# Attention products on two 64-row tiles of the matmul array, with chained passes and a reordered tail

## Chip, cores and metric

The kernel runs on one core of a Trainium2 chip. The metric is the device time of one execution in microseconds (us). The engines are named as in the profile: PE (TensorE, matmuls; PEld are its weight loads), DVE (VectorE), ACT (ScalarE), POOL (GpSimd), SP (SyncE, which only issues transfers here). Each works through its own list of instructions in order.

## The reference

```python
def _A_ref(x, k_cache, v_cache, wq, wo):          # 32 heads of 192, D = 640, Sq = Sk = 2048
    W = min(4096, max(256, Sk // 4))              # 512
    q = (x @ wq).reshape(B, Sq, Hq, Dh).transpose(0, 2, 1, 3)
    k, v = k_cache[:, :, Sk - W:, :], v_cache[:, :, Sk - W:, :]
    p = softmax(einsum("bhqd,bhkd->bhqk", q, k) * Dh ** -0.5)
    return einsum("bhqk,bhkd->bhqd", p, v) ... @ wo
def _B_ref(x, w_gate, w_up, w_down):              # F = 1536
    return (sigmoid(x @ w_gate) * (x @ w_up)) @ w_down
xn = layernorm(x)
out = x + _A_ref(xn, ...) * silu(_B_ref(xn, ...))
```

Inputs and output are bfloat16, sums are kept in float32.

## The kernel before

**Opening and gated block.** The 2048 rows are four blocks of 512 (`TB`), each four tiles of 128. Rows are normalised tile by tile (`stats_half`, `stats_end`, `normal`) and turned into `xnT`, on PE for the first block (`turn_pe`; the copies out of PSUM are L233 on DVE and L235 on ACT), by DMA for the others. `tile_gates` (L299) computes the first gates of block 0 tile by tile as the rows come; `gated` (L249) and `down` (L261) do the rest of the gated block and leave `gate`, the silu factor, for all rows. The loads of the opening are issued on SP and, the first gate weights alone, on ACT. At the end of this part the queries of the first two units are computed (L368), on all 128 rows of the array.

**Units.** The attention is cut into 32 units: 8 groups of 4 heads times 4 blocks of 512 queries; unit u is group `u // 4`, block `u % 4`. Each unit needs

- queries (`queries`, L420, evicted by DVE at L427): the contraction over 640 is done in halves of 64 rows, one on each half of the array, the two writing to the two 512-column halves of a PSUM bank pair. In a second pass the halves are exchanged. Between the passes DVE reads one column of the result into a tiny tile `seen` (L425), so that the second pass cannot begin before the first has landed;
- scores (`scores`, L402): heads of 192 in three pieces of 64, again two heads on the two halves of the array; ACT takes the exponential into `E` (L406);
- values (`values`, L436): the exponentials against `vbuf` (192 columns and one column of ones, 193), 16 matmuls a head on the whole array; DVE divides by the sum (L441, L442) into `o_st`;
- the turn of `o_st` into `oT` by four DMA transposes on SP (`turn_out`, L448);
- the projection (`project`, L475): for each of four row tiles, 6 chunks times (512 + 128) columns on the whole array, added by DVE into `acc` (L480, L482). For the last group but one, POOL also loads the row of x (L485, its own DMA queue), multiplies `acc` by `gate` (L486) and adds the row (L487). For the last group `finish_rows` multiplies the projection by `gate` into `o_sb` on DVE (L454; two buffers), adds `acc` (L455, on DVE or POOL) and issues the output (L456).

There are four PSUM bank pairs `bank[0..3]`, 1024 columns each. All of the order is written out by hand (manual schedule): every engine's list follows the order of the Python code.

**Main loop** (L494). 15 iterations of two units u0, u0+1. In the first half of each iteration the scores of these two units alternate with the passes of the queries of units u0+2, u0+3 (scores in banks 0 and 1, queries in 2 and 3); then come, in the second half, for eight heads in turn, one `values` and one `project` (of units u0-2, u0-1; none in the first iteration). The loads of the next group's wq, keys and values are issued on POOL, those of wo on SP.

**Tail** (L523). The scores of units 30 and 31 come in stretches of 6, 6 and 4, with the projections of unit 28 between them, two and two, their additions on DVE and outputs issued on POOL; then the projections of unit 29 (likewise), the values of 30 and 31, the projections of 30, and those of 31 in two halves of 320 columns (L467), each half finished by itself; these last additions are on POOL, for the last row tile on DVE.

Of the kernel before, what the change touches and what calls it, by code (L numbers as in the profile page):

```python
# [9 lines left out]
ALU = mybir.AluOpType  # L10
BF16 = mybir.dt.bfloat16
F32 = mybir.dt.float32
# [3 lines left out]
def kernel(  # L16
# [13 lines left out]
    nc = tc.nc  # L30
    P = 128
    H2 = 64

    xf = A_x.flatten_outer_dims()
# [36 lines left out]
    def wide(i):  # L71
        return bank[i][:].rearrange("p b n -> p (b n)")
# [17 lines left out]
    grp = {}  # L90
# [52 lines left out]
    with ExitStack() as bctx:  # L143
# [8 lines left out]

        xt = {}

        def load_x(t, n):

            x = xpool.tile([P, n, D], BF16, name=f"x_sb{n}", bufs=4 if n == 1 else 2)
            nc.sync.dma_start(x[:], xf[t * P:(t + n) * P, :].rearrange("(q p) d -> p q d", p=P))  # L158
            for i in range(n):
                xt[t + i] = x[:, i, :]  # L160

        def load_f(eng, w, r, f0, f1, c0=0, c1=NCD):
            eng.dma_start(w[:, c0:c1, f0 * P:f1 * P], r[:, c0:c1, f0 * P:f1 * P])

        nc.vector.memset(warm[:], 0.0)

        nc.vector.memset(wg_sb[:, 0, 0:2], 0.0)
        load_x(0, 1)
        load_x(1, 1)
        load_f(nc.scalar, wg_sb, wg_r, 0, 4)  # L170
        load_f(nc.sync, wu_sb, wu_r, 0, 4, 0, 3)
        load_x(2, 1)
        load_f(nc.sync, wu_sb, wu_r, 0, 4, 3, NCD)
# [20 lines left out]
        def stats_half(t, i):  # L194
            if i == 0:
                ln[t] = bwork.tile([P, 2, nc.vector.BN_STATS_DIM], F32, name="st")
            nc.vector.bn_stats(ln[t][:, i, :], xt[t][:, i * (D // 2):(i + 1) * (D // 2)])
# [15 lines left out]
        def normal(t, parts=((0, D),)):  # L213
            mv, rstd = ln[t]
            xn = xpool.tile([P, D], BF16, name="xn")
            for d0, d1 in parts:
                nc.vector.tensor_scalar(xn[:, d0:d1], xt[t][:, d0:d1], mv[:, 0:1], rstd[:, 0:1],
                                        op0=ALU.subtract, op1=ALU.mult)
            ln[t] = xn

        def turn_pe(t):

            engs = (nc.vector, nc.scalar) if t == 0 else (nc.scalar, nc.scalar)
            parts = []
            for i, (c0, c1) in enumerate(((0, 3), (3, NCD))):
                bk = bank[3][:, t % 2, :] if t or i == 0 else bank[2][:, 0, :]
                pT = bk[:, 0:NCD * H2].bitcast(BF16).rearrange("p (c n) -> p c n", c=NCD)
                for c in range(c0, c1):
                    nc.tensor.transpose(pT[:, c, :], ln[t][:, c * P:(c + 1) * P], ident[:])  # L229
                parts.append((engs[i], xnT[:, 0, c0:c1, t * P:(t + 1) * P], pT[:, c0:c1, :]))  # L230
            for eng, dst, src in parts:
                if eng is nc.vector:
                    nc.vector.tensor_copy(dst, src)  # L233
                else:
                    nc.scalar.activation(dst, src, AF.Copy)  # L235
# [75 lines left out]
        stats_half(0, 1)  # L311
        stats_end(0)
        normal(0, ((0, 3 * P), (3 * P, D)))
        turn_pe(0)
        dummy(2)
        stats_half(1, 1)
        stats_end(1)
        stats_half(2, 0)
        normal(1)
        stats_half(2, 1)  # L320
        stats_end(2)
        stats_half(3, 0)
# [67 lines left out]
    NU = NG * NB  # L390
    E = {}
    oT = {}
    seen = acc_pool.tile([P, DJ, 2], F32, name="seen")
    load_wo(0)

    def scores(u, pr, c, k):
# [32 lines left out]
    o_st = {}  # L429

    def values(u, h, k):
        e = E[u, h // 2]
        o4 = wide(k).rearrange("p (q n) -> p q n", q=TQ)
        for q in range(TQ):
            for c in range(KC):
                nc.tensor.matmul(o4[:, q, 0:DH + 1], lhsT=e[:, c, h % 2, q * P:(q + 1) * P],  # L436
                                 rhs=vbuf[:, h, c, 0:DH + 1], start=(c == 0), stop=(c == KC - 1))
        if h == 0:
            o_st[u] = o_pool.tile([P, TQ, GW], BF16, name="o_st")
        rden = small.tile([P, TQ, 1], F32, name="rden")  # L440
        nc.vector.reciprocal(rden[:], o4[:, :, DH:DH + 1])  # L441
        nc.vector.tensor_tensor(o_st[u][:, :, h * DH:(h + 1) * DH], o4[:, :, 0:DH],  # L442
                                rden[:].to_broadcast([P, TQ, DH]), ALU.mult)

    def turn_out(u):
        oT[u] = oT_pool.tile([P, GC, TB], BF16, name="oT")
        for q in range(TQ):
            nc.sync.dma_start_transpose(oT[u][:, :, q * P:(q + 1) * P], o_st[u][:, q, :])  # L448

    def finish_rows(t, d0, d1, src, add, out_eng):  # L450

        o_sb = fin.tile([P, D], F32, name="o_sb", bufs=2)[:, d0:d1]
        r_sb = gate[:, t, d0:d1]
        nc.vector.tensor_tensor(o_sb, src, r_sb, ALU.mult)  # L454
        add.tensor_tensor(r_sb, o_sb, acc[:, t, d0:d1], ALU.add)  # L455
        out_eng.dma_start(of[t * P:(t + 1) * P, d0:d1], r_sb)  # L456

    def project(u, q, k, out_eng, add=nc.vector):
        g, b = u // NB, u % NB
        wo = grp[g]["wo"]  # L460
        t = b * TQ + q
        if u == NU - 1:

            HD = D // 2
            for i in range(2):
                for cc in range(GC):
                    nc.tensor.matmul(bank[k[i]][:, 0, 0:HD],  # L467
                                     lhsT=oT[u][:, cc, q * P:(q + 1) * P],
                                     rhs=wo[:, cc, i * HD:(i + 1) * HD],
                                     start=(cc == 0), stop=(cc == GC - 1))  # L470
                finish_rows(t, i * HD, (i + 1) * HD, bank[k[i]][:, 0, 0:HD], add, out_eng[i])
            return
        for cc in range(GC):
            for d0, d1 in ((0, 512), (512, D)):
                nc.tensor.matmul(wide(k)[:, d0:d1], lhsT=oT[u][:, cc, q * P:(q + 1) * P],  # L475
                                 rhs=wo[:, cc, d0:d1], start=(cc == 0), stop=(cc == GC - 1))
        if g == NG - 1:
            finish_rows(t, 0, D, wide(k)[:, 0:D], add, out_eng)
        elif g == 0:
            nc.vector.tensor_copy(acc[:, t, :], wide(k)[:, 0:D])  # L480
        else:
            nc.vector.tensor_tensor(acc[:, t, :], wide(k)[:, 0:D], acc[:, t, :], ALU.add)  # L482
        if g == NG - 2:
            x_sb = fin.tile([P, D], BF16, name="row")
            nc.gpsimd.dma_start(x_sb[:], xf[t * P:(t + 1) * P, :])  # L485
            nc.gpsimd.tensor_tensor(acc[:, t, :], acc[:, t, :], gate[:, t, :], ALU.mult)  # L486
            nc.gpsimd.tensor_tensor(acc[:, t, :], acc[:, t, :], x_sb[:], ALU.add)  # L487

    sc = [(pr, c) for pr in range(2) for c in range(KC)]
    order = (2, 3, 0, 1)  # L490
# [3 lines left out]
    for u0 in range(0, NU - 2, 2):  # L494
        g, second = u0 // NB, u0 % NB != 0
        more = g + 1 < NG
        for u in (u0, u0 + 1):
            for i, what in enumerate(((0, 0), (1, 0), (0, 1), (1, 1), (2, 0), None, (2, 1), None)):
                scores(u, *sc[i], i % 2)
                if what is not None:  # L500
                    queries(u + 2, what[0], 2 + (what[0] + u) % 2, what[1])
        if more and not second:
            load_wq(g + 1, nc.gpsimd)
            load_keys(g + 1, nc.gpsimd)
        if more and second:
            turn_keys(g + 1)
        if not more:
            load_wo(g)
        for u in (u0, u0 + 1):
            for q in range(4):  # L510
                if u0 > 0:
                    values(u, q, order[2 * q % 4])
                    project(u - 2, q, order[(2 * q + 1) % 4], nc.sync)
                else:
                    values(u, q, order[q])
            turn_out(u)
        if more and second:
            load_values(g + 1, nc.gpsimd)
        if 0 < g < NG - 1 and not second:
            load_wo(g)  # L520


    u = NU - 2  # L523
    sc = [(v, *s) for v in (u, u + 1) for s in sc]
    for i in range(6):
        scores(*sc[i], order[i % 4])
    for q in range(2):
        project(u - 2, q, q, nc.gpsimd)
    for i in range(6, 12):
        scores(*sc[i], order[(i - 6) % 4])  # L530
    for q in range(2, 4):
        project(u - 2, q, q - 2, nc.gpsimd)
    for i in range(12, 16):
        scores(*sc[i], order[i % 4])
    for q in range(4):
        project(u - 1, q, order[q], nc.gpsimd)
    for v in (u, u + 1):
        for h in range(4):
            values(v, h, order[h])
        turn_out(v)  # L540
    for q in range(4):
        project(u, q, order[q], nc.sync, nc.gpsimd if q < 3 else nc.vector)
    for q in range(4):
        i = 2 * q % 4
        project(u + 1, q, order[i:i + 2], (nc.scalar, nc.sync), nc.gpsimd if q < 3 else nc.vector)


# [28 lines left out]
```

The softmax here doesn't subtract the row's maximum and nothing guards it: scores larger than these inputs give would overflow.

## Time and profile before

| what | us |
|---|---|
| median of 6 runs (lowest to highest) | 927.64 (927.22 to 931.09) |
| the profiled execution | 927.22 |
| its span, first to last instruction | 925.4 |
| PE busy | 914.4 (99%) |
| DVE, ACT, POOL busy | 463.3, 302.7, 139.8 |
| scores L402, queries L420 (busy of the group) | 198.4, 223.7 |
| values L436, projection L475 (busy of the group) | 189.5, 197.9 |
| one iteration of the main loop (start of values 801.30 to 848.53) | 47.23 |
| tail, from its first scores to the end of the last matmuls | 872.3 to 920 |

The granted clock of PE is 0.999 of full speed on average. Busy times of PE are sums over pipelined matmuls, of which each record (376 ns for 512 columns) is longer than the distance from one to the next; distances between starts are what counts. In the timeline a line is a merged run of like instructions: start, duration, engine, source line, operation, tiles, rows of the array, shape and count; in brackets is the idle time of the engine before it and what ended it.

### The profile page before, as it was taken

Reading aid. Unit: us, or ns where it says so; the run is one execution under the profiler, and the core shown is the slowest. Engines: PE = TensorE matmul, PEld = TensorE weight load, DVE = VectorE, ACT = ScalarE, POOL = GpSimd, SP = SyncE. Lnnn points to the kernel's source line nnn. Section 1 sums busy time; section 2 is a strip of 40 time slices with the busy share of each in tenths; the row PEclk is TensorE's granted clock in tenths of the full one; section 3 lists DMA queues with packets and bytes.
Section 4 is the critical chain, followed back from the end, with each engine's and each line's share of the span. In section 5 each row is a group of like instructions: output and inputs, shape, how many; then the busy total and the mean of one; then the engine's idle time right before and its main releaser. Section 6 shows DMA issues by size and latency. Waiting matters only on the chain.

```text
span 925.4 us, 17975 instructions
## 1 busy us (share of the span) xinstructions
PE 914.4 (99%) x7926; PEld 547.9 (59%) x8004; DVE 463.3 (50%) x734; ACT 302.7 (33%) x333; POOL 139.8 (15%) x169
## 2 busy tenths in 40 slices
PE   9999999999999999999999999999999999999997
PEld 6445455465757565656565656566666656565665
DVE  5452522444545454645454545545554545454566
ACT  4222222245151514242424233333324242415240
POOL 1000100011002000200020012001100110175744
PEclk9999999999999999999999999999999999999999
DMA  9310330114424232333433252415251415252625
GB/s 321 78 29 1 89 86 1 43 61 86 86 53 112 77 77 62 103 86 50 88 94 96 43 95 78 111 36 103 77 112 29 110 61 98 67 118 92 109 67 126
DMA packets 162334, 76.68 MB, mean 83 GB/s; under 512 B 140976, under 2 KB 157568, under 8 KB 162256
## 3 DMA queue, kind: packets, MB, share of 16 engines
q1 hardware_dynamic: 154832, 52.72, 26.2%
q0 software_dynamic: 6192, 21.83, 8.1%
q8 instruction: 62, 1.02, 0.5%
q10 hardware_dynamic: 1232, 0.98, 0.3%
q14 instruction: 16, 0.13, 0.1%
HBM read 39.45 MB, written 2.62 MB: 45 GB/s over the span
## 4 chain that ended last, share of the span: by engine, by line
PE 97%; issue 1%; DMA 1%; POOL 0%; DVE 0%; SPq 0%; ACT 0%; DVEq 0%
PE bank L475 22%; PE bank L420 21%; PE bank L436 19%; PE bank L402 18%; PE bank L249 10%; PE bank L261 6%; PE bank L368 1%; PE bank L299 1%; DMA x_sb<-in_A_x_dram 1%; POOL gate L455 0%; DVE o_sb L454 0%; PE bank L229 0%; SPq L158 0%; DVE gate L455 0%; ACT xnT L235 0%
## 5 line engine op out<-in xcount | busy, mean ns | idle before, releaser
L406 ACT ACTIVATE E<-bank 128x1024 bf16<-128x1024 f32 x256 | 255.7, 1024 | 456.8 <-PE bank L402 456.7
L420 PE MATMUL bank<-xnT,wq_sb 64*128 64x512 bf16 x1800 | 223.7, 376 | 0.0
L475 PE MATMUL bank<-wo_sb,oT 128*128 128x512 bf16 (+1 forms) x1288 | 197.9, 296 | 3.0
L402 PE MATMUL bank<-qT,kT 64*128 64x512 bf16 x1536 | 198.4, 376 | 0.0
L436 PE MATMUL bank<-vbuf,E 128*128 128x193 bf16 x2048 | 189.5, 247 | 0.0
L436 PEld LDWEIGHTS <-E 128*128 128x128 bf16 x2048 | 168.6, 98 | 18.0 <-issue 6.4
L427 DVE CAST qT<-bank 128x1024 bf16<-128x1024 f32 x90 | 110.2, 1225 | 128.5 <-PE bank L420 128.5
L475 PEld LDWEIGHTS <-oT 128*128 128x128 bf16 x1488 | 117.3, 98 | 75.4 <-issue 1.3
L420 PEld LDWEIGHTS <-wq_sb 64*128 64x128 bf16 x1800 | 93.1, 100 | 102.2
L402 PEld LDWEIGHTS <-kT 64*128 64x128 bf16 x1536 | 74.0, 94 | 89.8 <-issue 4.8
L442 DVE TENSOR_TENSOR o_st<-bank,rden 128x768 bf16<-128x768 f32 x128 | 122.5, 957 | 4.4
L482 DVE TENSOR_TENSOR acc<-bank,acc 128x640 f32<-128x640 f32 x96 | 79.2, 825 | 43.4 <-PE bank L475 43.2
L118 POOL DMA_DIRECT2D vbuf<-in_A_v_cache_dram x28 | 21.1, 753 | 308.0 <-PE bank L436 305.1
L425 DVE COPY seen<-bank 128x2 f32<-128x2 f32 x90 | 14.4, 159 | 93.8 <-PE bank L420 93.8
L441 DVE RECIPROCAL rden<-bank 128x4 f32<-128x4 f32 x128 | 23.4, 182 | 65.1 <-PE bank L436 65.1
L249 PE MATMUL bank<-xnT,wg_sb 128*128 128x512 bf16 x216 | 54.5, 379 | 0.2
L249 PE MATMUL bank<-xnT,wu_sb 128*128 128x512 bf16 x215 | 54.4, 379 | 0.3
L261 PE MATMUL bank<-wd_sb,hT 128*128 128x128 bf16 (+1 forms) x376 | 52.4, 297 | 0.4
L255 DVE TENSOR_TENSOR hT<-bank,sig 128x512 bf16<-128x512 f32 x44 | 30.3, 689 | 42.8 <-ACT sig L252 42.8
L252 ACT ACTIVATE sig<-bank 128x512 bf16<-128x512 f32 x44 | 26.3, 597 | 68.4 <-PE bank L249 65.3
L261 PEld LDWEIGHTS <-hT 128*128 128x128 bf16 x384 | 29.7, 98 | 23.1
L97 POOL DMA_DIRECT2D wq_sb<-in_A_wq_dram x7 | 6.3, 898 | 221.0 <-PE bank L420 221.0
(55 smaller groups left out, 346.2 us busy)
## 6 DMA issues: line engine op xcount, KB each, us to landing
wo_sb<-in_A_wo_dram SPq DMA_DIRECT2D x7, 960.0 KB, 5.3
wq_sb<-in_A_wq_dram POOLq DMA_DIRECT2D x7, 960.0 KB, 5.9
k_st<-in_A_k_cache_dram POOLq DMA_DIRECT2D x14, 384.0 KB, 5.5
vbuf<-in_A_v_cache_dram POOLq DMA_DIRECT2D x28, 192.0 KB, 3.2
row<-in_A_x_dram POOLq DMA_DIRECT2D x16, 160.0 KB, 2.6
oT<-o_st SPq DMA_TRANSPOSE x128, 2.6
x_sb<-in_A_x_dram SPq DMA_DIRECT2D x3, 640.0 KB, 10.4
wd_sb<-in_B_w_down_dram SPq DMA_DIRECT2D x1, 1920.0 KB, 14.3
```

Source lines behind the costliest of these rows:

```text
L249: nc.tensor.matmul(bank[k][:, half, 0:r1 - r0], lhsT=w[:, c, f * P:(f + 1) * P], rhs=xnT[:, b, c, r0:r1], start=(c == 0), stop=(c == NCD - 1))
L252: nc.scalar.activation(sig[:, 0:r1 - r0], bank[k][:, 0, 0:r1 - r0], AF.Sigmoid)
L255: nc.vector.tensor_tensor(hT[b][:, f, r0:r1], bank[k][:, 1, 0:r1 - r0], sig[:, 0:r1 - r0], ALU.mult)
L261: nc.tensor.matmul(wide(k)[:, d0:d1], lhsT=hT[b][:, f, q * P:(q + 1) * P], rhs=wd_sb[:, f, d0:d1], start=(f == 0), stop=(f == NF - 1))
L402: nc.tensor.matmul(bank[k][:, i, :], lhsT=kT[r, pr, j, c * P:(c + 1) * P], rhs=q[r, pr * DJ + j, :], start=(j == 0), stop=(j == DJ - 1))
L406: nc.scalar.activation(E[u, pr][:, c, :, :], bank[k][:], AF.Exp, scale=scale_qk)
L420: nc.tensor.matmul(bank[k][:, half, :], lhsT=wq[r, c, col:col + DJ * (P - 1) + 1:DJ], rhs=xnT[r, b, c, :], start=(c == 0 and not second), ...
L427: nc.vector.tensor_copy(qT[u][:, 2 * m:2 * m + 2, :], bank[k][:])
L436: nc.tensor.matmul(o4[:, q, 0:DH + 1], lhsT=e[:, c, h % 2, q * P:(q + 1) * P], rhs=vbuf[:, h, c, 0:DH + 1], start=(c == 0), stop=(c == KC ...
L442: nc.vector.tensor_tensor(o_st[u][:, :, h * DH:(h + 1) * DH], o4[:, :, 0:DH], rden[:].to_broadcast([P, TQ, DH]), ALU.mult)
L475: nc.tensor.matmul(wide(k)[:, d0:d1], lhsT=oT[u][:, cc, q * P:(q + 1) * P], rhs=wo[:, cc, d0:d1], start=(cc == 0), stop=(cc == GC - 1))
L482: nc.vector.tensor_tensor(acc[:, t, :], wide(k)[:, 0:D], acc[:, t, :], ALU.add)
```

## The change

1. `values` and `project` are done like `queries`: each product is cut into two halves of 64 rows, which run on the two halves of the array and write to the two halves of the bank pair, in two passes with the halves exchanged; a copy of one column of each half into `seen` stands between the passes. A projection's 640 columns are now twice 320. Both become generators that yield after each pass.
2. `flow` chains them: the first pass of the next job stands before the second pass of this one. `pairs` interleaves two jobs pass by pass.
3. In the first half of an iteration, a pass of the queries now stands ahead of the scores, not behind.
4. The tail: scores of unit 30 alternate with the passes of unit 28's projections (additions now on POOL, outputs on SP), scores of unit 31 with the passes of unit 30's values; then values of 31, projections of 29 and of 30, all chained; then the last rows, still on the whole array, with five of the eight additions on POOL (six before).
5. The opening: the first gate weights go in two parts on SP, tile 1 of x on ACT; a small memset goes; tile 1's second statistics stand ahead of `turn_pe(0)`, its normalisation ahead of tile 2's statistics.

```diff
-        load_x(1, 1)
-        load_f(nc.scalar, wg_sb, wg_r, 0, 4)
+        load_x(1, 1, nc.scalar)
+        load_f(nc.sync, wg_sb, wg_r, 0, 4, 0, 3)
+        load_f(nc.sync, wg_sb, wg_r, 0, 4, 3, NCD)
...
+        stats_half(1, 1)
         turn_pe(0)
         dummy(2)
-        stats_half(1, 1)
         stats_end(1)
+        normal(1)
         stats_half(2, 0)
-        normal(1)
...
     def values(u, h, k):
-        for q in range(TQ):
-            for c in range(KC):
-                nc.tensor.matmul(o4[:, q, 0:DH + 1], lhsT=e[:, c, h % 2, q * P:(q + 1) * P],
-                                 rhs=vbuf[:, h, c, 0:DH + 1], start=(c == 0), stop=(c == KC - 1))
+        for turn in range(2):
+            for qq in range(TQ // 2):
+                for c in range(KC):
+                    for i in range(2):
+                        r = slice(i * H2, (i + 1) * H2)
+                        q = (i ^ turn) * (TQ // 2) + qq
+                        nc.tensor.matmul(o4[:, q, 0:DH + 1],
+                                         lhsT=e[r, c, h % 2, q * P:(q + 1) * P],
+                                         rhs=vbuf[r, h, c, 0:DH + 1],
+                                         start=(turn == 0 and qq == 0 and c == 0),
+                                         stop=(turn == 1 and c == KC - 1), skip_group_check=True)
+            if turn == 0:
+                nc.vector.tensor_copy(seen[:, DJ, :], bank[k][:, :, 0])
+                yield
...
     def project(u, q, k, out_eng=None, add=nc.vector):
+        res = bank[k][:, :, 0:HD]
+        for turn in range(2):
+            for cc in range(GC):
+                for i in range(2):
+                    r = slice(i * H2, (i + 1) * H2)
+                    half = i ^ turn
+                    nc.tensor.matmul(res[:, half, :], lhsT=oT[u][r, cc, q * P:(q + 1) * P],
+                                     rhs=wo[r, cc, half * HD:(half + 1) * HD],
...
+            if turn == 0:
+                nc.vector.tensor_copy(seen[:, DJ + 1, :], bank[k][:, :, 0])
+                yield
...
+    def flow(jobs):
+        before = None
+        for j in jobs:
+            next(j)
+            if before is not None:
+                next(before)
+            before = j
+        next(before)
+
+    def pairs(jobs):
+        for i in range(0, len(jobs), 2):
+            for _ in range(2):
+                for j in jobs[i:i + 2]:
+                    yield next(j)
...
-                scores(u, *sc[i], i % 2)
                 if what is not None:
                     queries(u + 2, what[0], 2 + (what[0] + u) % 2, what[1])
+                scores(u, *sc[i], i % 2)
...
+    passes = pairs([project(u - 2, q, 2 + q % 2, nc.sync, nc.gpsimd) for q in range(4)])
+    for i in range(8):
+        scores(u, *sc[i], i % 2)
+        next(passes)
+    passes = pairs([values(u, h, 2 + h % 2) for h in range(4)])
+    for i in range(8):
+        scores(u + 1, *sc[i], i % 2)
+        next(passes)
+    flow([values(u + 1, h, h) for h in range(4)]
+         + [project(u - 1, q, q, nc.scalar, nc.gpsimd) for q in range(4)]
+         + [project(u, q, q, nc.sync, nc.gpsimd if q < 3 else nc.vector) for q in range(4)])
     for q in range(4):
-        project(u, q, order[q], nc.sync, nc.gpsimd if q < 3 else nc.vector)
-    for q in range(4):
-        i = 2 * q % 4
-        project(u + 1, q, order[i:i + 2], (nc.scalar, nc.sync), nc.gpsimd if q < 3 else nc.vector)
+        last_rows(q)
```

More of the change, by code (lines that the diff above doesn't have):

```diff
@@ L153, with load_x @@
         xt = {}
-        def load_x(t, n):
+        def load_x(t, n, eng=nc.sync):
             x = xpool.tile([P, n, D], BF16, name=f"x_sb{n}", bufs=4 if n == 1 else 2)
-            nc.sync.dma_start(x[:], xf[t * P:(t + n) * P, :].rearrange("(q p) d -> p q d", p=P))
+            eng.dma_start(x[:], xf[t * P:(t + n) * P, :].rearrange("(q p) d -> p q d", p=P))
             for i in range(n):
@@ L165 @@
         nc.vector.memset(warm[:], 0.0)
-        nc.vector.memset(wg_sb[:, 0, 0:2], 0.0)
         load_x(0, 1)
-        load_x(1, 1)
-        load_f(nc.scalar, wg_sb, wg_r, 0, 4)
+        load_x(1, 1, nc.scalar)
+        load_f(nc.sync, wg_sb, wg_r, 0, 4, 0, 3)
+        load_f(nc.sync, wg_sb, wg_r, 0, 4, 3, NCD)
         load_f(nc.sync, wu_sb, wu_r, 0, 4, 0, 3)
@@ L392 @@
     oT = {}
-    seen = acc_pool.tile([P, DJ, 2], F32, name="seen")
+    seen = acc_pool.tile([P, DJ + 2, 2], F32, name="seen")
     load_wo(0)
@@ L443, in values @@
                                 rden[:].to_broadcast([P, TQ, DH]), ALU.mult)
+        if h == 3:
+            turn_out(u)
+        yield
     def turn_out(u):
@@ L448, in turn_out, with cols, finish_rows, project @@
             nc.sync.dma_start_transpose(oT[u][:, :, q * P:(q + 1) * P], o_st[u][:, q, :])
-    def finish_rows(t, d0, d1, src, add, out_eng):
+    HD = D // 2
+    def cols(x):
+        return x.rearrange("p (i n) -> p i n", i=2)
+    def finish_rows(t, d0, d1, form, src, add, out_eng):
         o_sb = fin.tile([P, D], F32, name="o_sb", bufs=2)[:, d0:d1]
         r_sb = gate[:, t, d0:d1]
-        nc.vector.tensor_tensor(o_sb, src, r_sb, ALU.mult)
+        nc.vector.tensor_tensor(form(o_sb), src, form(r_sb), ALU.mult)
         add.tensor_tensor(r_sb, o_sb, acc[:, t, d0:d1], ALU.add)
         out_eng.dma_start(of[t * P:(t + 1) * P, d0:d1], r_sb)
-    def project(u, q, k, out_eng, add=nc.vector):
+    def project(u, q, k, out_eng=None, add=nc.vector):
         g, b = u // NB, u % NB
@@ L461, in project @@
         t = b * TQ + q
[L462 to L476, printed above, removed]
+        res = bank[k][:, :, 0:HD]
[6 more added lines that the diff above has]
+                                     rhs=wo[r, cc, half * HD:(half + 1) * HD],
+                                     start=(turn == 0 and cc == 0),
+                                     stop=(turn == 1 and cc == GC - 1), skip_group_check=True)
+            if turn == 0:
+                nc.vector.tensor_copy(seen[:, DJ + 1, :], bank[k][:, :, 0])
+                yield
         if g == NG - 1:
-            finish_rows(t, 0, D, wide(k)[:, 0:D], add, out_eng)
+            finish_rows(t, 0, D, cols, res, add, out_eng)
         elif g == 0:
-            nc.vector.tensor_copy(acc[:, t, :], wide(k)[:, 0:D])
+            nc.vector.tensor_copy(cols(acc[:, t, :]), res)
         else:
-            nc.vector.tensor_tensor(acc[:, t, :], wide(k)[:, 0:D], acc[:, t, :], ALU.add)
+            nc.vector.tensor_tensor(cols(acc[:, t, :]), res, cols(acc[:, t, :]), ALU.add)
         if g == NG - 2:
@@ L487, in project, with last_rows @@
             nc.gpsimd.tensor_tensor(acc[:, t, :], acc[:, t, :], x_sb[:], ALU.add)
+        yield
+    def last_rows(q):
+        u = NU - 1
+        t = (NB - 1) * TQ + q
+        for i in range(2):
+            k = (2 * q + i) % 4
+            for cc in range(GC):
+                nc.tensor.matmul(bank[k][:, 0, 0:HD], lhsT=oT[u][:, cc, q * P:(q + 1) * P],
+                                 rhs=grp[NG - 1]["wo"][:, cc, i * HD:(i + 1) * HD],
+                                 start=(cc == 0), stop=(cc == GC - 1))
+            finish_rows(t, i * HD, (i + 1) * HD, lambda x: x, bank[k][:, 0, 0:HD],
+                        nc.gpsimd if 2 * q + i < 5 else nc.vector, (nc.scalar, nc.sync)[i])
+    def flow(jobs):
[11 more added lines that the diff above has]
+                    yield next(j)
     sc = [(pr, c) for pr in range(2) for c in range(KC)]
@@ L508 @@
             load_wo(g)
+        jobs = []
         for u in (u0, u0 + 1):
@@ L511 @@
                 if u0 > 0:
-                    values(u, q, order[2 * q % 4])
-                    project(u - 2, q, order[(2 * q + 1) % 4], nc.sync)
-                else:
-                    values(u, q, order[q])
-            turn_out(u)
+                    jobs.append(values(u, q, order[2 * q % 4]))
+                    jobs.append(project(u - 2, q, order[(2 * q + 1) % 4], nc.sync))
+                else:
+                    jobs.append(values(u, q, order[q]))
+        flow(jobs)
         if more and second:
@@ L523 @@
     u = NU - 2
[L524 to L534, printed above, removed]
-    for q in range(4):
[L536 to L540, printed above, removed]
-    for q in range(4):
-        project(u, q, order[q], nc.sync, nc.gpsimd if q < 3 else nc.vector)
-    for q in range(4):
-        i = 2 * q % 4
-        project(u + 1, q, order[i:i + 2], (nc.scalar, nc.sync), nc.gpsimd if q < 3 else nc.vector)
+    passes = pairs([project(u - 2, q, 2 + q % 2, nc.sync, nc.gpsimd) for q in range(4)])
[9 more added lines that the diff above has]
+         + [project(u, q, q, nc.sync, nc.gpsimd if q < 3 else nc.vector) for q in range(4)])
+    for q in range(4):
+        last_rows(q)
 _INS = ['A_x', 'A_k_cache', 'A_v_cache', 'A_wq', 'A_wo', 'B_x', 'B_w_gate', 'B_w_up', 'B_w_down']
```

## Prediction

> **What bounds the kernel now.** I read the page first: busy times, then the chain of work that ended last.
>
> ```profile
> PE 914.4 (99%) x7926; PEld 547.9 (59%) x8004; DVE 463.3 (50%) x734; ACT 302.7 (33%) x333; POOL 139.8 (15%) x169
> ...
> PE 97%; issue 1%; DMA 1%; POOL 0%; DVE 0%; SPq 0%; ACT 0%; DVEq 0%
> ```
>
> TensorE (PE) is the chain almost from end to end, so only what shortens PE's own list, or makes PE wait, moves the time. A share of 99% cannot tell a matmul from a pause inside a run of matmuls, so I went on to the timeline of PE (start, duration of the merged run, engine, line, shapes, count). First a stretch of score and query matmuls, then the tail:
>
> ```profile
> 825.05 0.82 PE L402 MATMUL bank<-qT,kT 64*128 64x512 bf16 x6
> 825.71 1.24 PE L420 MATMUL bank<-xnT,wq_sb 64*128 64x512 bf16 x10
> 826.79 0.81 PE L402 MATMUL bank<-qT,kT 64*128 64x512 bf16 x6
> 827.43 1.24 PE L420 MATMUL bank<-xnT,wq_sb 64*128 64x512 bf16 x10
> ...
> 872.28 4.06 PE L402 MATMUL bank<-qT,kT 64*128 64x512 bf16 x36
> 876.27 3.43 PE L475 MATMUL bank<-wo_last,oT 128*128 128x512 bf16 x23
> 879.64 4.06 PE L402 MATMUL bank<-qT,kT 64*128 64x512 bf16 x36
> ...
> 896.22 10.83 PE L436 MATMUL bank<-vbuf,E 128*128 128x193 bf16 x128
> 906.89 6.68 PE L475 MATMUL bank<-wo_last,oT 128*128 128x512 bf16 x47
> 913.41 6.68 PE L467 MATMUL bank<-wo_last,oT 128*128 128x320 bf16 x48
> ```
>
> From start to start: five pairs of 64-row matmuls of 512 columns take 1.08 us, three take 0.64, so a pair takes **0.2155**; the full-array matmul of 512 columns (L249) takes the same. Values take 10.67/128 = **0.0833** each (193 columns). A projection step of 640 columns takes 6.52/24 = **0.2717**, and 320 columns in the last rows 0.136. So two half-array matmuls together are no faster than one whole one; this change cannot win by pace.
>
> What it can win is the **switch** between the forms. 18 pairs of scores should take 3.88 us; the projections start 3.99 after them: 0.11 lost. The 12 steps back take 3.37 instead of 3.26: 0.11 again. Start times of single matmuls say 0.308 instead of 0.212 at the step to 128 rows (and 0.012 at the next matmul) and 0.152 instead of 0.056 at the step back: 0.10 each on average.
>
> **The change, part by part.** The profiled run took 927.22 us (span 925.4 and 1.8 around it), 0.4 below the median 927.64. I add to 927.2.
>
> *1. No switches.* To 128 rows: 15 iterations and 3 times in the tail; back: after L368, 15 times, 2 in the tail; 36. Two stay (after L368, and into last_rows). 34 x 0.10 = **-3.5** (-3.7 to -3.2).
>
> *2. Pace of the pairs.* A projection has 12 pairs of 320 columns: 12 x 0.136 = 1.63, as 6 x 0.2717 does now. Values have 16 pairs of 193 columns a head where 16 whole matmuls stand, 2048 in all. No row shows a pair so short. Lower end: 193/512 of the 512-column pair, 0.0812, 2048 x 0.0021 = -4.3. Upper end: a load and a matmul come every 0.056 us in the opening (L299: 20 in 1.11); if the two halves took turns at that, 0.112 a pair, +59. In the pairs at hand the two loads start 2 ns apart and both last 94 to 101 ns, beside each other; the nearest row for 193 columns is the whole matmul: 0.0833, **0**.
> [...]
>
> *3. The copies into seen.* 128 for values and 124 for projections at 0.16 us (L425): 40 us more on DVE, which is at 463 of 925. They lie beside PE. In a period of 2.96 us (a head and a projection) DVE does 0.18 + 0.96 + 0.82 + 2 x 0.16 = 2.28. A second pass waits for its copy. DVE takes up a result some 0.2 us after its last matmul; by then it may be evicting the head before, until about 1.37 us into the period, so the copy ends at 1.55, and PE wants it at 2.30. Cover 0.75 us for values, 0.95 for projections: **0**. Were it gone, each head would cost what is missing. With heads alone (first iteration, last unit) DVE needs 1.38 a head against PE's 1.33; over 8 heads 0.4 behind: still covered.
>
> *4. Queries ahead of scores.* The same matmuls. ACT's 1.02 per score group stays ahead of PE, the query banks (2, 3) have long been emptied, and wq is needed 0.65 us earlier, some 17 us after it lands: **0**.
>
> *5. Opening.* The second statistics of tile 1 now stand ahead of the copy L233, which moves from 5.83 to 6.00, and the first gates from 6.25 to about 6.45. In return tile 1's normalisation no longer stands behind x tile 2 (landed 7.48), so its turn comes at 8.21 instead of 8.41, and the second tile starts at 9.24 instead of 9.44. The loads move about as many bytes ahead of x tile 2. **-0.2** (-0.5 to +0.4).
>
> *6. The last rows.* DVE now also does the sixth half's addition (0.5 us) ahead of the seventh's product, POOL one less; the buffers of o_sb (two) still chain DVE to POOL at 0.83 a half: **+0.3** (-0.5 to +1). The outputs go from POOL's queue to SP's and ACT's; behind them on SP stand the transposes of unit 30, ready some 6 us later; on ACT nothing but outputs. oT of unit 31 must wait for the projections of unit 29, and has 5.7 us to land against 2.6.
>
> *7. Where it is paid: unit 28's rows in the tail.* Its additions (L455) move from DVE to POOL. POOL's own timeline from the last iteration on:
>
> ```profile
> 852.55 1.39 POOL L486 TENSOR_TENSOR acc<-acc,gate 128x640 f32<-128x640 f32 x1 [10.45 <-DVE acc L482]
> ...
> 876.46 1.41 POOL L486 TENSOR_TENSOR acc<-acc,gate 128x640 f32<-128x640 f32 x1
> 880.95 1.90 POOL L487 TENSOR_TENSOR acc<-acc,row 128x640 f32<-128x640 f32 x1 [3.08 <-DMA row<-in_A_x_dram]
> 882.80 0.58 POOL L485 DMA_DIRECT2D row<-in_A_x_dram  x1
> 883.39 1.41 POOL L486 TENSOR_TENSOR acc<-acc,gate 128x640 f32<-128x640 f32 x1
> 885.46 1.39 POOL L487 TENSOR_TENSOR acc<-acc,row 128x640 f32<-128x640 f32 x1 [0.65 <-DMA row<-in_A_x_dram]
> ```
>
> POOL is **behind**: its eight rounds (issue a row, multiply, wait, add) last from 852.55 to 886.85, 34.3 us, 14.5 us into the tail that begins at 872.35. One iteration earlier they took 33.3. Today nobody waits for that; after the change unit 28's additions queue behind it. In the new kernel the first round starts 4.74 us after the values phase (first projection done at 3.63, then 1.11 as now), the phase lasts 8 x 2.96 = 23.7, so POOL comes free 4.74 + 33.3 to 34.3 - 23.7 = 14.3 to 15.3 into the tail. Its first addition takes 1.54: 15.9 to 16.9. o_sb has two buffers, so the third product waits for that and ends (0.9) at 16.8 to 17.8. It is what empties bank 2, and bank 2 takes the first values of unit 30, which PE reaches after 8 x (0.647 + 0.815) + 0.647 = 12.35. PE waits 4.5 to 5.4; bank 3 follows one POOL addition later, 0.26 more. **+5.2** (4.5 to 5.7; 3.9 if POOL made its fastest rounds).
>
> *8. The clock after that wait.* PE's last matmul starts at 919.8; then:
>
> ```profile
> 920.00:924.40 4.40, 0.09 (x1) 0.00 (x0) 1.99 (x4) 0.00 (x0) 0.81 (x1) 1.00 0.31 93
> 924.50:925.40 0.90, 0.00 (x0) 0.00 (x0) 0.00 (x0) 0.00 (x0) 0.00 (x0) 0.50 0.00 0
> ```
>
> (the column of 1.00 and 0.50 is the granted clock.) It fell about 4.5 us after the last work, and a wait of 4.5 to 5.4 may just reach that. Coming back: in the opening 256 columns took 0.213 (half pace) and full pace was there at the first gates, 5.1 us after the first matmul; half of that is 2.5. So 0 to 2.5; I take **+1.0**, between fall and no fall.
> [...]
>
> Sum: 927.2 - 3.5 + 0 - 0.2 + 0.3 + 5.2 + 1.0 = **930.0**.
>
> **Rivals.**
> A. *No wait in the tail.* If POOL's rows are done by 10 us into the tail, or DVE finds a free o_sb: 927.2 - 3.5 - 0.2 + 0.3 = **923.8**. For it: the switches are certain. Against it: the backlog of two iterations and the third product's dependence on POOL.
> B. *PE's instructions come too slowly*: the case that is clearly slower. A head and a projection today are 56 loads and matmuls in 2.96 us; afterwards 112, one every 26.5 ns. The densest row, L299, shows 28 ns (two in 0.056). It decides from 26.5 ns on (for the 12 heads without a projection from 1.33/64 = 20.8); at 28 each period takes 3.14, so 112 x 0.17 = 19, the 12 heads add 12 x 0.46 = 5.5, and the wait in the tail shrinks by the longer phase to some 3.8: 927.2 - 3.5 + 0.1 + 24.5 + 3.8 = **952**; at 27 about 940. For it: nothing in the trace is denser. Against it: L299 is held by its 128 columns, so 28 is only what was asked.
> C. *The switch stays*, if the drain belongs to a change of half and not of form: 933.5. Against it: scores and queries alternate halves with no gap.
>
> **Numbers.** Forecast 0.62 (927 to 933.5), A 0.18, B 0.17, C 0.03. What can be told from no change is 0.3%, 924.9 to 930.4. The forecast with the clock kept gives about 929, within; with the fall 930 to 932, mostly beyond: 0.34 same, 0.28 slower. Faster is A less 0.01: 0.17; same 0.35; slower 0.28 + 0.17 + 0.03 = 0.48. The range takes in A, the forecast's ends and the mild part of B: 923.5 to 935.
>
> **What would show it.** 64-row value pairs 0.083 apart and an iteration of 47.0 us instead of 47.23 (steps 1, 2); no PE wait for seen; one PE wait of some 5 us for bank 2, released by DVE's o_sb, which itself waits for POOL's gate, and perhaps PEclk below 9 in the slice after it. I am wrong if value pairs stand clearly over 0.083 apart, or if the tail has no such wait.

## Result, and the profile after

| | us |
|---|---|
| median before / after (38 and 17 runs) | 927.64 / 931.75 |
| ratio of the runs | 1.0042, 95% interval 1.0033 to 1.0051 |
| runs after, lowest to highest | 928.78 to 934.88 |
| the profiled execution after, its span | 933.68, 931.9 |

The change makes the kernel 0.4% slower, and spreads its runs over 6 us (before: 4). The page after, first the busy times, then the chain:

```profile
PE 916.1 (98%) x11522; PEld 630.8 (68%) x11540; DVE 485.3 (52%) x978; ACT 302.4 (32%) x333; POOL 146.3 (16%) x168
...
PE 82%; DMA 6%; issue 5%; POOL 4%; DVE 1%; ACT 0%; POOLq 0%
```

Before, the chain was PE to 97%. Now DMA, POOL and "issue" have 15% of it: the chain that ends last runs for a long stretch over POOL and the rows of x that POOL loads and waits for. The matmuls themselves pace as the whole ones did. PE's timeline of one iteration (start, duration of the run, shapes, count):

```profile
704.21 0.61 PE L401 MATMUL bank<-qT,kT 64*128 64x512 bf16 x4
704.64 0.85 PE L441 MATMUL bank<-vbuf,E 64*128 64x193 bf16 x16
705.31 0.99 PE L489 MATMUL bank<-wo_sb,oT 64*128 64x320 bf16 x12
706.13 1.51 PE L441 MATMUL bank<-vbuf,E 64*128 64x193 bf16 x32
707.46 1.81 PE L489 MATMUL bank<-wo_sb,oT 64*128 64x320 bf16 x24
```

Eight value pairs take 0.67 (0.0833 a pair), six projection pairs 0.82. The values start 0.43 after the last two pairs of scores, which is what two pairs take: nothing is lost on the way in. Before, three pairs of scores, 0.65 by their pace, took 0.74 there:

```profile
706.03 0.81 PE L402 MATMUL bank<-qT,kT 64*128 64x512 bf16 x6
706.77 1.51 PE L436 MATMUL bank<-vbuf,E 128*128 128x193 bf16 x16
```

An iteration takes 47.02 us (751.66 to 798.68 between the starts of values) where it took 47.23. The tail then loses what the loop won. POOL, DVE and PE in the tail, which begins at 870.03 (in brackets the idle time of the engine before, and what ended it):

```profile
885.90 1.39 POOL L506 TENSOR_TENSOR acc<-acc,row 128x640 f32<-128x640 f32 x1 [0.62 <-DMA row<-in_A_x_dram]
887.25 6.00 POOL L475 TENSOR_TENSOR gate<-o_sb,acc 128x640 bf16<-128x640 f32 x4
...
888.80 0.82 DVE L474 TENSOR_TENSOR o_sb<-bank,gate 128x640 f32<-128x640 f32 x1 [9.62 <-POOL gate L475]
889.68 1.48 PE L441 MATMUL bank<-vbuf,E 64*128 64x193 bf16 x16 [7.13 <-DVE o_sb L474]
```

POOL's backlog of rows ends at 887.25, 17.2 us into the tail; its first addition for unit 28 frees a buffer of o_sb; DVE, idle for 9.62, makes the third product; only that empties bank 2, for which PE has stood for **7.13 us**. Then look at the duration of PE's 16 matmuls: 1.48 instead of the 0.84 that the same line takes a few microseconds later. The windows tell why (length, busy times of PE, PEld, DVE, ACT, POOL, then the granted clock):

```profile
882.70:886.50 3.80, 0.00 (x0) 0.00 (x0) 0.00 (x0) 0.98 (x1) 3.17 (x4) 1.00 0.14 43
886.70:889.60 2.90, 0.00 (x0) 0.00 (x0) 0.80 (x1) 0.00 (x0) 2.90 (x3) 0.50 0.00 0
889.70:893.40 3.70, 3.70 (x38) 2.93 (x39) 0.98 (x2) 0.93 (x1) 3.55 (x3) 0.50 0.37 130
893.50:897.20 3.70, 3.70 (x66) 2.74 (x63) 2.15 (x5) 2.23 (x3) 0.00 (x0) 1.00 0.13 44
```

The clock fell to half while PE waited (at 886.61, 4.05 us after PE's last matmul ended) and came back at 893.44, 3.76 us after PE had work again: 38 matmuls in the third window, 66 in the fourth. That is 1.9 us more. Fall and return are 6.83 us apart.

### The profile page after: what moved, and what is told of

The parts are those of the page before. It is cut to its first block, busy times and chain, and to the rows that moved or that the text cites. A ratio compares the mean times of both kernels' runs of the same rounds, so it can differ in the third digit from the quotient of the medians.

```text
span 931.9 us, 25362 instructions
## 1 busy us (share of the span) xinstructions
PE 916.1 (98%) x11522; PEld 630.8 (68%) x11540; DVE 485.3 (52%) x978; ACT 302.4 (32%) x333; POOL 146.3 (16%) x168
## 4 chain that ended last, share of the span: by engine, by line
PE 82%; DMA 6%; issue 5%; POOL 4%; DVE 1%; ACT 0%; POOLq 0%
PE bank L419 18%; PE bank L489 17%; PE bank L441 15%; PE bank L401 15%; PE bank L248 10%; PE bank L260 6%; DMA row<-in_A_x_dram 5%; POOL acc L506 2%; PE bank L367 1%; DMA k_st<-in_A_k_cache_dram 1%; PE bank L298 1%; POOL gate L475 1%; DVE o_sb L474 0%; POOL k_perm L110 0%; POOL vbuf L118 0%
## 5 line engine op out<-in xcount | busy, mean ns | idle before, releaser
L419 PE MATMUL bank<-xnT,wq_sb 64*128 64x512 bf16 x1800 | 226.4, 376 | 0.0
L489 PE MATMUL bank<-wo_sb,oT 64*128 64x320 bf16 x2688 | 205.2, 296 | 0.0
L441 PE MATMUL bank<-vbuf,E 64*128 64x193 bf16 x4096 | 196.5, 244 | 7.1 <-DVE o_sb L474 7.1
L401 PE MATMUL bank<-qT,kT 64*128 64x512 bf16 x1536 | 201.4, 377 | 0.5 <-DVE o_st L454 0.5
L441 PEld LDWEIGHTS <-E 64*128 64x128 bf16 x4096 | 179.8, 94 | 17.9 <-issue 8.3
L489 PEld LDWEIGHTS <-oT 64*128 64x128 bf16 x2976 | 164.6, 94 | 29.2
L419 PEld LDWEIGHTS <-wq_sb 64*128 64x128 bf16 x1800 | 105.9, 100 | 87.2 <-issue 0.4
L401 PEld LDWEIGHTS <-kT 64*128 64x128 bf16 x1536 | 88.3, 94 | 74.3 <-issue 0.9
L118 POOL DMA_DIRECT2D vbuf<-in_A_v_cache_dram x28 | 21.1, 753 | 315.1 <-PE bank L441 312.1
```

Source lines behind the costliest of these rows:

```text
L401: nc.tensor.matmul(bank[k][:, i, :], lhsT=kT[r, pr, j, c * P:(c + 1) * P], rhs=q[r, pr * DJ + j, :], start=(j == 0), stop=(j == DJ - 1))
L419: nc.tensor.matmul(bank[k][:, half, :], lhsT=wq[r, c, col:col + DJ * (P - 1) + 1:DJ], rhs=xnT[r, b, c, :], start=(c == 0 and not second), ...
L441: nc.tensor.matmul(o4[:, q, 0:DH + 1], lhsT=e[r, c, h % 2, q * P:(q + 1) * P], rhs=vbuf[r, h, c, 0:DH + 1], start=(turn == 0 and qq == 0 a ...
L489: nc.tensor.matmul(res[:, half, :], lhsT=oT[u][r, cc, q * P:(q + 1) * P], rhs=wo[r, cc, half * HD:(half + 1) * HD], start=(turn == 0 and c ...
```

## Experiments

Theory T: the 64-row passes gain what the switches cost; the new tail makes PE wait for POOL's backlog, and the clock falls in that wait. Rival R1: the passes and their copies cost the time themselves. Rival R2: the interleaved tail is slow in itself. All times below are medians. Each run below stands with its ratio to the kernel before on the same chip.

**e1: unit 28's additions back on DVE**

```diff
-    passes = pairs([project(u - 2, q, 2 + q % 2, nc.sync, nc.gpsimd) for q in range(4)])
+    passes = pairs([project(u - 2, q, 2 + q % 2, nc.sync, nc.vector) for q in range(4)])
```

> The changed kernel with one edit: unit 28's four additions in the tail back on DVE. Theory T (the loss is POOL's backlog: PE waits 7.1 us for bank 2 behind it and then runs 3.8 us at half clock; the 64-row passes themselves gain): the wait for bank 2 and the fall of the clock both go, 931.75 - 7.1 - 1.9 = about 923 to 925, faster than before. Rival R1 (the passes and their copies into seen cost the time, the wait only uncovers it): it stays within 1 us of 931.75, with waits elsewhere in the tail. Rival R2 (the interleaved tail is slow by itself, since DVE must now do the additions beside the values): 927 to 929.

Measured: 925.13 us, ratio 0.9972 (0.9961 to 0.9983), all runs from 924.48 to 925.45. That is 0.1 over what T expected. One word takes 6.6 us off the changed kernel and makes it faster than before; PE's values of unit 30 now follow the scores (start 882.24) with no idle time:

```profile
882.88 0.85 PE L441 MATMUL bank<-vbuf,E 64*128 64x193 bf16 x16
```

R1 and R2 fall.

**e2: two more buffers, the additions still on POOL**

```diff
+    spare = {}
     def finish_rows(t, d0, d1, form, src, add, out_eng):
-        o_sb = fin.tile([P, D], F32, name="o_sb", bufs=2)[:, d0:d1]
+        if t in spare:
+            o_sb = spare[t]
+        else:
+            o_sb = fin.tile([P, D], F32, name="o_sb", bufs=2)[:, d0:d1]
...
     u = NU - 2
+    o_x = load1.tile([P, 2, D], F32, name="o_x", tag="k_perm")
+    spare[2], spare[3] = o_x[:, 0, :], o_x[:, 1, :]
```

> The changed kernel with two more buffers for the products o_sb of unit 28's third and fourth row tile (in the place of a key tile that is no longer used); the additions stay on POOL, and POOL stays as late as it is. T: DVE no longer waits for POOL, bank 2 is emptied in time, no wait of PE and no fall of the clock, 923 to 925, with POOL's additions still ending some 20 us into the tail. If POOL's lateness delays something else as well (the outputs, the projections of unit 29), a part of the loss stays: over 926. R1: within 1 us of 931.75.

Measured: 924.66 us, ratio 0.9970 (0.9960 to 0.9981). POOL is as late as ever, and nobody waits for it. Timelines of DVE, PE and POOL; the tail of this run begins at 870.5:

```profile
882.44 0.82 DVE L479 TENSOR_TENSOR o_x<-bank,gate 128x640 f32<-128x640 f32 x1 [0.57 <-PE bank L494]
882.87 0.84 PE L441 MATMUL bank<-vbuf,E 64*128 64x193 bf16 x16
...
887.56 3.03 POOL L480 TENSOR_TENSOR gate<-o_sb,acc 128x640 bf16<-128x640 f32 x2
```

The values start with no idle time at 882.87; POOL's first addition comes at 887.56. So it isn't POOL's lateness by itself that costs, but that a PSUM bank hung on it through two buffers.

**e3: that one part alone, in the kernel before**

```diff
-        project(u - 2, q, q, nc.gpsimd)
+        project(u - 2, q, q, nc.sync, nc.gpsimd)
...
-        project(u - 2, q, q - 2, nc.gpsimd)
+        project(u - 2, q, q - 2, nc.sync, nc.gpsimd)
```

> The kernel before with one part of the change alone: unit 28's additions on POOL and their outputs on SP. T: DVE's third product waits for POOL, which comes free 14.5 us into the tail; banks 0 and 1, which the scores 15 and 16 take, are emptied late: two waits of about 1 us each, 929 to 930, and no fall of the clock. If the place of the additions doesn't matter: 927.6.

Measured: 928.84 us, ratio 1.0012 (1.0003 to 1.0020); a little under what T expected, on its side. The waits of PE there (total, times, longest):

```profile
PE bank L402 <- DVE o_sb L454: 1.3, 2, 0.7
```

Two waits, as expected; they took 0.65 each instead of some 1 us. The clock kept full speed up to 926.49, after the last matmuls. The same move costs 1.3 us in the old tail and some 6.6 in the new one, where bank 2 is wanted sooner.

**e4: the main loop's part alone** (the opening and the tail of before, the tail's products on the whole array; the edit is the diff of `values`, `project`, `flow` and the loop in the change above)

> The kernel before with the change in the main loop alone (64-row passes, chained, queries ahead of scores); opening and tail as before, the tail's products on the whole array. T: 13 iterations of 47.02 instead of 47.23 (-2.8), 0.15 in the first iteration and 0.1 at the entry of the tail: 924.4 to 925. R1: at or over 927.6.

Measured: 924.42 us, ratio 0.9968 (0.9957 to 0.9980); iterations of 47.02. T's number; R1 said 927.6 or more.

**e8: switches put back, 16 an iteration** (from e4)

```diff
     def values(u, h, k):
...
-        for turn in range(2):
-            for qq in range(TQ // 2):
-                for c in range(KC):
-                    for i in range(2):
...
+        yield
+        for q in range(TQ):
+            for c in range(KC):
+                nc.tensor.matmul(o4[:, q, 0:DH + 1], lhsT=e[:, c, h % 2, q * P:(q + 1) * P],
+                                 rhs=vbuf[:, h, c, 0:DH + 1], start=(c == 0), stop=(c == KC - 1))
```

> The kernel with the changed main loop alone, but with the values back on the whole array and in one pass, between the two passes of a projection: 16 switches of form in an iteration that has none now. T (what the loop gained is the switches, 0.10 to 0.11 each): 14 x 16 x 0.105 = 23.5 us more than the loop alone, 948, an iteration of 48.7. If the gain was the chained passes or the order of queries: little change, 924 to 927.

Measured: 951.12 us, ratio 1.0255 (1.0241 to 1.0269): 26.7 us over e4, 23.5 expected. Its PE at the start of an iteration's second half:

```profile
869.85 0.81 PE L402 MATMUL bank<-qT,kT 64*128 64x512 bf16 x6
870.69 0.99 PE L480 MATMUL bank<-wo_sb,oT 64*128 64x320 bf16 x12
871.61 1.51 PE L439 MATMUL bank<-vbuf,E 128*128 128x193 bf16 x16
873.05 1.80 PE L480 MATMUL bank<-wo_sb,oT 64*128 64x320 bf16 x24
874.78 1.51 PE L439 MATMUL bank<-vbuf,E 128*128 128x193 bf16 x16
```

A projection pass takes 0.92 instead of 0.82, the head 1.44 instead of 1.33: 0.10 and 0.11, each a switch. Eight heads make 1.7; 0.2 more is lost at the entry, where the first projection pass now stands directly behind the scores (0.84 from their start instead of 0.65). It starts at 870.69, just after DVE has copied the last queries out of the bank that it takes (869.41 to 870.64); in the changed loop a pass of the values stands between. The loss at the entry was not in my expectation; the price of a switch was.

**e9 and e5: the wait filled with work** (38 and 56 matmuls of zeros, ahead of the values that wait)

```diff
         scores(u + 1, *sc[i], i % 2)
+        if i == 0:
+            dummy(38)
         next(passes)
```

> The changed kernel with 56 unneeded matmuls (256 columns, about 0.107 us each, 6.0 us in all) into bank 1 just before the values of unit 30 that wait for bank 2. They add 6.0 us of work to PE where it is idle for about 7.1. T: the wait shrinks to 1 us, the clock doesn't fall, and what the fall cost comes back: 1.5 to 2 us less than the changed kernel, 929.5 to 930.3, although PE does 6 us more. If the clock's fall cost nothing: 931.75 or more.

> As the busy wait before, with 38 unneeded matmuls (4.1 us) in the place of 56, whose 6.3 us outlasted the wait: bank 2 was free 5.1 us after PE came to it in that trace. Now the matmuls lie inside the wait, which therefore keeps its length, and only the clock's fall is taken away: the difference to the changed kernel is what the fall costs. T: 1 to 2 us less than 931.75, 929.8 to 930.8, with a narrower spread of runs. If the fall costs nothing: 931.75.

Measured: e5 931.42 us, ratio 1.0039 (1.0026 to 1.0051); e9 929.60, ratio 1.0027 (1.0015 to 1.0038). e5 missed its number: in that run bank 2 was free 5.1 us after PE came to it, not 7.1, so that 6.3 us of matmuls outlasted the wait, and the time is simply e1 and 6.3. e9 was made for that. Its dummies, and what was left of the wait:

```profile
882.72 4.32 PE L188 MATMUL bank<-warm 128*128 128x256 bf16 x38
...
887.62 0.84 PE L441 MATMUL bank<-vbuf,E 64*128 64x193 bf16 x16 [0.58 <-DVE o_sb L474]
```

The wait is 4.9 us from PE's coming (882.7 to 887.6), the first value pass runs at full pace (0.84), and eight of ten runs lie within 928.9 and 930.0 (two at 933 and 934, so the whole spread is not narrower). In this run the clock stays full from 5.6 us to 927.2. 38 useless matmuls make the kernel some 2.1 us faster by the medians, 1.4 by the ratios (1 to 2 expected). This is an estimate of what the fall of the clock costs in a typical run, not a clear result: the intervals of the ratios overlap, and the wait itself differs from run to run.

**e10: the rows of x on another queue**

```diff
-            nc.gpsimd.dma_start(x_sb[:], xf[t * P:(t + 1) * P, :])
+            nc.sync.dma_start(x_sb[:], xf[t * P:(t + 1) * P, :])
```

> The changed kernel with the rows of x for POOL's last step loaded from SP's queue, where POOL waits for each row that it has issued itself now. POOL's round is then 1.41 + 1.39 and the gaps, some 2.9 us, against one projection each 2.96 us: POOL keeps pace, comes free 2 to 4 us into the tail, and its additions for unit 28 are in time. T: no wait for bank 2, 924.5 to 925.5. If POOL stays late for another reason (its own pace beside a busier DVE), a wait stays: over 927.

Measured: 926.55 us, ratio 0.9988 (0.9979 to 0.9997). The wait was not gone but 0.64 us:

```profile
868.48 1.40 POOL L506 TENSOR_TENSOR acc<-acc,row 128x640 f32<-128x640 f32 x1 [5.95 <-DMA row<-in_A_x_dram]
...
884.98 0.84 PE L441 MATMUL bank<-vbuf,E 64*128 64x193 bf16 x16 [0.64 <-DVE o_sb L474]
```

With the row at hand POOL's round took 2.9 us, but POOL waited 5.95 us for one row: SP issued it at 865.94, behind four transposes (860.21 to 865.81). POOL was free at 882.5, 10.7 us into the tail. So half of the expectation failed, and the time lies between the two that were named; the dependence on how late POOL is (15 to 17 us: waits of 4.9 to 7.1; 10.7: 0.6) is T's.

**e6: the opening alone** (the opening's lines of the change, in the kernel before)

> The kernel before with the new opening alone. The trace of the changed kernel has the first gated block 0.14 us later than before, as tile 0 of x landed 0.57 later: 927.6 to 928, no difference that can be told. My recorded -0.2 would give 927.4, also not to be told in the time; the start of the first gated block tells (16.70 before).

Measured: 927.94 us, ratio 1.0002 (0.9993 to 1.0011): no difference that the time can tell. In its profiled run the gated block began at 18.69, some 2 us late, in e10 (the same opening) at 18.62 and in e4 (the old one) at 19.24. These three go with the clock: its record begins, at full, only at 10.4 us in e6 and e10 (35 and 37 matmuls ran in the 4 us up to 10.0, 61 in the 3.5 us from 10.5 on), in the other runs between 3.9 and 6.8; and in e4 it fell back to half from 7.3 to 10.8. Without the three, the block began at 16.70 to 17.00 in four traces with the old opening and at 16.84 to 17.46 in five with the new: 0.3 us later on average, though the two overlap.

**e7: mended** (e1, the opening of before, and the tail's banks shifted by two)

```diff
-    passes = pairs([project(u - 2, q, 2 + q % 2, nc.sync, nc.gpsimd) for q in range(4)])
+    passes = pairs([project(u - 2, q, q % 2, nc.sync, nc.vector) for q in range(4)])
...
-        scores(u, *sc[i], i % 2)
+        scores(u, *sc[i], 2 + i % 2)
...
-    passes = pairs([values(u, h, 2 + h % 2) for h in range(4)])
+    passes = pairs([values(u, h, h % 2) for h in range(4)])
...
-    flow([values(u + 1, h, h) for h in range(4)]
+    flow([values(u + 1, h, order[h]) for h in range(4)]
...
```

> The changed kernel with three things mended: unit 28's additions on DVE, the tail's banks shifted by two (so that its first scores don't wait for bank 0, 0.63 us in the trace), the opening as before. T: 925.1 of the kernel with DVE additions, less 0.6, less 0.1: 924.2 to 924.6, faster than both kernels. If the bank shift only moves the wait to the next pass: 925.

Measured: 923.93 us, ratio 0.9959 (0.9946 to 0.9973), all runs within 923.81 and 924.18: the fastest of all, 3.6 us under before and 0.3 under what was expected. The wait for bank 0 is gone: scores follow the last projection pass by 0.82, as they should:

```profile
868.74 0.99 PE L490 MATMUL bank<-wo_sb,oT 64*128 64x320 bf16 x12
869.56 0.83 PE L402 MATMUL bank<-qT,kT 64*128 64x512 bf16 x6
```

## Why the prediction was right, step by step

*1, switches (-3.5): right.* (34 x 0.10 is 3.4; the 0.21 that an iteration with two switches lost makes 0.105 each, 3.6 in all.) The loop alone gave -3.1 by the medians, with the tail -3.6 (e7); the price of one switch is confirmed by e8.

*2, pace of pairs (0): right.* 0.0833 for 193 columns. The upper end (the halves in turn) and rival B (instructions too slow) are out: in the heads of the first iteration a load or matmul comes every 21 ns. Eight of these heads took 10.83 us, against 10.78 with one switch before; what 10.83 has over 128 x 0.0833 is one wait of 0.17, told under 3. Two weight loads go into each 83 ns there, side by side.

*3, copies into seen (0): right but for two waits.* Where heads and projections alternate, PE waits for no copy. Of eight heads without projections the last has only one pass to cover its copy, and "still covered" failed there. DVE's copy ends at 210.45, and PE goes on at 210.51, 0.17 late (the gap stands at PE's loads):

```profile
210.30 0.15 DVE L448 COPY seen<-bank 128x2 f32<-128x2 f32 x1
210.51 0.61 PEld L441 LDWEIGHTS <-E 64*128 64x128 bf16 x15 [0.16 <-issue]
```

The same wait comes once more in the tail, among the values of unit 31 (at 902.87): 0.3 in all. DVE's busy time rose by 22 us, where I had 40.

*4, queries ahead of scores (0): right in the loop.* But where no queries stand ahead, at the entry of the tail, the first scores take bank 0 from the last head one projection pass after it. I had not looked there:

```profile
868.59 0.99 PE L489 MATMUL bank<-wo_sb,oT 64*128 64x320 bf16 x12
870.03 0.82 PE L401 MATMUL bank<-qT,kT 64*128 64x512 bf16 x6 [0.45 <-DVE o_st L454]
```

1.44 from start to start instead of 0.82: a missed term of +0.6, mended in e7.

*5, opening (-0.2): wrong sign, within its bounds.* The step that failed was "the loads move about as many bytes": tile 0 of x was hit. With tile 1 issued at the same moment from ACT, DVE's first statistics came at 3.74 instead of 3.17. That is not the luck of one run: they start at 3.09 to 3.26 in the five traces with the old opening and at 3.61 to 3.98 in the seven with the new. In the profiled run 0.43 of the 0.57 us had been made up when the gated block began, at 16.84 instead of 16.70. The time shows no difference (e6).

*6, last rows (+0.3): nothing there.* From the first of the last matmuls to the end of the span 11.9 us (920.01 to 931.9) against 12.0.

*7, the wait (+5.2): the mechanism right, in the profiled run undersized.* It was 7.13 there, 5.1 in e5 and 4.9 in e9, where I had 4.5 to 5.4. POOL's first round began 4.76 after the values phase, as worked out (4.74). Undersized was the length of the rounds, 36.8 instead of 33.3 to 34.3, because rows landed later; in e5 and e9 the rounds took 34.6 and 34.5, and the waits lie in my range. The waits for rows, before and after:

```profile
POOL acc L487 <- DMA row<-in_A_x_dram: 14.5, 14, 3.1
```

```profile
POOL acc L506 <- DMA row<-in_A_x_dram: 21.2, 14, 3.7
```

Between the runs of the experiments this sum goes from 15.6 (e9) to 21.1 (e2) with the same loop. What sets it stays open.

*8, the clock (+1.0 out of 0 to 2.5): right in kind.* 1.9 in the profiled run; e9 gives 1.4 to 2.1 as an estimate for a typical one. The fall comes in some runs and not in others, as the forecast allowed, and probably in more than half. Of the 17 runs eleven show a mean granted clock of 0.996 or less and took 931.5 to 934.9; six show 0.997 or 0.998 and took 928.8 to 931.2. A fall like the profiled one takes 0.0037 off this mean, so the eleven probably had it. How much of the difference in time is the clock, and how much a longer wait that made it fall, these means don't tell.

For the profiled run the terms as measured add up: 927.2 - 3.6 + 0.1 (opening) + 0.6 (bank 0) + 0.3 (copies) - 0.1 (last rows) + 7.1 + 1.9 = 933.5, against 933.68. The sum of the forecast missed the median by 1.75: 0.9 of it are the two forgotten waits, at bank 0 and for the copies; the rest, by subtraction, lies in the wait and the clock. Rival A's time, 923.8, is about what the kernel takes when bank 2 doesn't hang on POOL (e1, e2, e7: 923.9 to 925.1). Rival C fell with e4.

## What to carry to other kernels

A price is paid where the next user of a buffer stands, not where the slow engine is: before work is moved to an engine with idle time, look how far behind it is at that place of its list, and what its result releases (here: addition, buffer, product, PSUM bank, matmul). An engine idle in 84% of the span was 15 to 17 us late at the one place that mattered. And a gain of many small terms (34 switches, 3.6 us) is lost to a single wait in the tail; look at the two ends of the kernel before the loop.

## What the runs showed of the hardware

- A change between matmuls of 64 and of 128 rows took 0.10 us of PE each way (e8: 0.10 and 0.11; before: 0.308 instead of 0.212 from start to start, 0.152 instead of 0.056).
- Pairs of 64-row matmuls with 193 and 320 columns (after) and with 512 (before) took 0.0833, 0.136 and 0.2155 us, as long as one 128-row matmul of that width (before: 0.0833, 0.136, 0.2155); neither a gain nor a loss.
- In a wait of PE of 7.1 us (after) the granted clock went to half after 4.05 us, for 6.83 us, of which 3.76 had work; in waits of 0.6 us (e3, e10) it did not.
